# The expert output product as a sixth chunk of the last part's Strassen step

## The chip, the cores and the metric

The kernel runs on one core of a Trainium2 chip. The core has five engines with instruction streams of their own: TensorE (matmuls, PE in the profile; PEld is its weight load), VectorE (DVE), ScalarE (ACT), GpSimd (POOL) and SyncE (SP), which here only issues DMAs. The metric is the device time of one execution in microseconds. Before the change three runs took 771.34, 771.65 and 771.67 us; their median is 771.65.

## What is computed

For 2048 tokens x (width 640) the output is `g * a + (1 - g) * b`, with one gate `g` per token. Part `a` is the real part of a two-dimensional Fourier transform, written as matrix products; part `b` is a layer of 256 experts, of which every token picks two in each of 32 heads by two key scores:

```python
g = _sigmoid((x * gate_w).sum(-1, keepdims=True))
y = jnp.einsum("ts,bse->bte", dft_seq_re, a) - jnp.einsum("ts,bse->bte", dft_seq_im, b)
act = _gelu(jnp.einsum("nd,nhkd->nhk", xf, ue))
out = jnp.einsum("nhk,nhk,nhkd->nd", g, act, ve)
```

Written densely, the expert part is a matrix z (2048 tokens x 256 experts: activation times summed gate weights times 1 - g) times v (256 x 640). That last product, z times v, is what the change is about.

## The kernel before, in words

All matmuls are single-precision values split in two (`split`, lines 120 to 124): a high part made by ACT's copy and a low part made by a subtraction on POOL or VectorE. `mm3` (lines 126 to 130) then issues three 128x512 matmuls for one product, so all of them show as lines 128, 129 and 130.

The work is staged by hand in one program order. First come 128 pieces (`NPC`) of the transform along the sequence: for each of two matrices and four column chunks of 512 tokens, 16 pieces of 15 matmuls (`seq_piece`). When the 16 pieces of a chunk are done, its five banks are copied out by ACT (line 222), multiplied by the gate on VectorE (`gate_piece`, line 193) and stored to DRAM as `pd` (`store_piece`, line 203). The last of these, piece group 7, is gated in slot NPC and its five stores are issued in slot NPC+1 on SP; those of the other groups are issued on ACT. Between the pieces run the score matmuls, the picks, and `experts`, which builds the summed gate weights per expert with short TensorE products (line 653, out of tiles called hot), masked copies on ACT (line 612) and reductions on VectorE (line 618). `Pump` feeds this background work by credits, and all of it is issued before the last part begins.

What else is to be done at a certain place is registered with `at(n, f, ...)` and runs, in the order of registration, when slot n of the program has been issued (`follow`). Slots below NPC are pieces, slots from NPC on are the steps of the last part.

The last part multiplies the stored, gated partial results (4 chunks of 512 tokens, real and imaginary, 5 chunks of 128 columns as the contraction) by the transform of the width. It works in two halves b = 0, 1. In a half the left side is a 2x2 arrangement (two token chunks by real and imaginary), the right side D a 2x2 arrangement (real and imaginary by two column groups of 256), and a Strassen step with seven products forms four output quarters out of seven units instead of eight:

```python
UNITS = ("a11", "a12", "s1", "s2", "s4", "s3", "a22")
```

The last 128 columns (bank W) are left over and go along as a third product in the units a11, a12, s1 and a22. The sums on the left (s1 to s4) are made of stored sums (`pqs`) in half 0 and on VectorE (`add_a`, line 801) in half 1; the sums on the right, P, are made once by `make_sums` and `split_sums` in VectorE and POOL, for each of the 5 chunks, in the slots NPC-14 to NPC-5. `NSTEP` is the number of steps of a half, 7 units times 5 chunks; a step has 9 matmuls (with W) or 6 (s2, s4, s3). The step's operands lie in a ring of six slots and are split five steps ahead (`AHEAD`, `split_step`): by ACT and POOL, and by ACT and VectorE for s2 and s3. The first five are split in the slots NPC-4 to NPC-1 (`prep_split`).

The raw operands come by `load_a` on SP's queue into tiles that `take` hands out in a fixed order and `give` returns: 5 of the tag wf (the buffers of the pieces before), 12 of X10 to X15 (which the pieces free one by one) and 2 of xf, 19 in all; after that, returned ones.

The expert product is made beside this, without Strassen. `load_v` (NPC-3) loads v, `split_v` (NPC) splits it on ACT and VectorE and makes a negated copy of the last columns on ACT (line 765). For each of the four chunks of 512 tokens `load_z` issues eleven DMAs on SP (the gate row, line 861; the activations, line 864; the summed weights in four pieces, line 867, each for two expert halves), `split_z` multiplies them on VectorE (one operation at line 877, two each at lines 880 and 881) and splits them into `zop` by ACT and POOL. In a half, chunk 0 is loaded in slot M-1 and split at M+3 (M is the half's first slot), chunk 1 at M+21 and M+25. `z_group` issues the matmuls in four places: 18 at the end of unit a12, 12 at the end of s4, 12 after s3 (`quarter`, with its own subtraction in `post`, "q"), and 18 ahead of a22. `store_gates(1)`, which writes the second group's summed weights to DRAM, is registered at NPC+28.

The queues matter: every engine and SP's DMA queue work strictly in the order in which the program issued. A DMA whose tile is not yet free, or whose source is not yet computed, holds up all DMAs behind it on SP.

## Time and profile before

| | |
|---|---|
| median of three runs | 771.65 us |
| profiled execution | 771.14 us, its span 769.4 us |
| PE busy | 764.3 us (99%), 4125 matmuls |
| DVE, ACT, POOL busy | 544.8 us (71%), 314.0 us (41%), 333.1 us (43%) |
| granted TensorE clock | 1.000 |
| last part | from 614.94 us to 765.4 us |

The span goes from the first to the last instruction; the profiled execution's time has 1.74 us more around it. A line of a timeline has the start, the duration, the engine, the kernel's line, the operation and its operands; what stands in brackets is the idle time before it and what ended it. `x5` means that five like instructions in a row are shown as one, with the time from the first's start to the last's end. SPq is SP's DMA queue: the time of such a line is that of issuing, not of the transfer. In a table by stages each engine has its busy time and, in brackets, its instructions. A busy PE is not a PE at its peak: a matmul shows as 0.39 us and the next begins 0.23 us after it.

### The profile page before, as it was taken

How to read it: one execution, taken by the hardware profiler on the slowest of the kernel's cores; microseconds unless marked ns; L12 is line 12 of the kernel's file. 1: busy time of each engine (PE TensorE's matmuls, PEld its weight loads, DVE VectorE, ACT ScalarE, POOL GpSimd, SP SyncE). 2: the span in 40 equal slices, each digit the busy share in tenths (PEclk: the TensorE clock that was granted, in tenths of full speed). 3: DMA queues.
4: the chain of work that ended last, by engine and by line, in shares of the span. 5: the costliest groups of instructions: out<-in, count | busy, mean ns of one | idle time of the engine just before them, and what ended most of it. 6: DMA issues, size and time to landing. Idle time of an engine off the chain costs nothing.

```text
span 769.4 us, 11163 instructions
## 1 busy us (share of the span) xinstructions
PE 764.3 (99%) x4125; PEld 625.1 (81%) x4125; DVE 544.8 (71%) x628; ACT 314.0 (41%) x572; POOL 333.1 (43%) x232
## 2 busy tenths in 40 slices
PE   9999999999999999999999999999999999999997
PEld 7777777888888888888888888888888878888886
DVE  7751032289899799999899969869889862427551
ACT  5334223321223532533523675543345663424350
POOL 5423225232422323324156656334357574549270
PEclk9999999999999999999999999999999999999999
DMA  9977995403212332221353442558864677766321
GB/s 344 347 294 187 357 345 203 150 27 97 77 40 73 115 116 59 65 96 47 100 170 125 153 148 83 167 191 287 276 222 166 221 266 250 243 195 199 124 83 68
DMA packets 75654, 130.33 MB, mean 169 GB/s; under 512 B 17104, under 2 KB 24400, under 8 KB 75344
## 3 DMA queue, kind: packets, MB, share of 16 engines
q1 hardware_dynamic: 63424, 113.23, 44.5%
q10 hardware_dynamic: 12176, 16.40, 6.0%
q8 instruction: 32, 0.52, 0.3%
q14 instruction: 22, 0.18, 0.1%
HBM read 102.84 MB, written 25.17 MB: 166 GB/s over the span
## 4 chain that ended last, share of the span: by engine, by line
PE 97%; POOL 1%; DMA 1%; issue 0%; SPq 0%; DVE 0%; DVEq 0%; POOLq 0%
PE b L128 31%; PE b L130 30%; PE b L129 30%; PE b L333 2%; PE b L215 2%; PE b L653 1%; DMA ra<-pqs 1%; POOL WS L124 1%; PE b L344 1%; PE b L283 0%; POOL WP L124 0%; SPq L798 0%; DVE ST L1002 0%; DVEq L1108 0%; POOLq L124 0%
## 5 line engine op out<-in xcount | busy, mean ns | idle before, releaser
L124 POOL TENSOR_TENSOR WS<-wf,WS 128x512 fp32r<-128x512 f32 x127 | 194.0, 1531 | 258.6 <-ACT WS L123 246.5
L128 PE MATMUL b<-WS,X 128*128 128x512 f32 x620 | 244.2, 394 | 0.0
L130 PE MATMUL b<-WS,X 128*128 128x512 f32 x620 | 241.5, 389 | 0.0
L129 PE MATMUL b<-WS,X 128*128 128x512 f32 x620 | 241.4, 389 | 0.0
L128 PEld LDWEIGHTS b<-WS,X 128*128 128x128 f32 x620 | 116.3, 188 | 28.5 <-issue 4.1
L130 PEld LDWEIGHTS b<-WS,X 128*128 128x128 f32 x620 | 116.4, 188 | 24.6
L129 PEld LDWEIGHTS b<-WS,X 128*128 128x128 f32 x620 | 116.4, 188 | 23.4
L123 ACT ACTIVATE WS<-wf 128x512 fp32r<-128x512 f32 x127 | 80.2, 632 | 95.6 <-PE b L130 52.8
L642 DVE TENSOR_TENSOR hot<-rows,wtab 128x1024 f16<-128x1024 f16 x64 | 63.2, 1014 | 10.2 <-PE b L653 10.2
L438 ACT ACTIVATE sc<-b 128x512 f32<-128x512 f32 x32 | 19.8, 618 | 107.6 <-PE b L130 107.6
L128 PE MATMUL b<-WU,xh 128*128 128x512 f32 x160 | 62.3, 390 | 0.0
L129 PE MATMUL b<-WU,xh 128*128 128x512 f32 x160 | 62.3, 390 | 0.0
L130 PE MATMUL b<-WU,xl 128*128 128x512 f32 x160 | 62.2, 389 | 0.0
L124 POOL TENSOR_TENSOR xl<-xf,xh 128x640 fp32r<-128x640 f32 x16 | 25.8, 1615 | 82.8 <-ACT xh L123 78.5
L452 DVE TENSOR_REDUCE mm<-sc 128x64 f32<-128x1024 f32 x32 | 38.9, 1217 | 25.7 <-ACT sc L438 25.1
L124 POOL TENSOR_TENSOR WS<-ra,WS 128x512 fp32r<-128x512 f32 x32 | 44.6, 1410 | 25.5 <-ACT WS L123 25.3
L454 DVE TENSOR_TENSOR eq<-sc,mm 128x1024 f16<-128x1024 f32 x32 | 51.5, 1608 | 1.1
L612 ACT ACTIVATE b<-b,mask 128x128 f32<-128x128 f32 x128 | 42.6, 340 | 16.0 <-PE b L653 12.9
L347 DVE TENSOR_TENSOR WU<-b,WU 128x512 fp32r<-128x512 f32 (+1 forms) x16 | 7.9, 491 | 57.5 <-ACT WU L346 57.5
L124 POOL TENSOR_TENSOR WP<-ra,WP 128x512 fp32r<-128x512 f32 x18 | 27.6, 1543 | 34.1 <-ACT WP L123 27.8
L458 DVE TENSOR_REDUCE rr<-eq 128x64 f16<-128x1024 f16 x32 | 39.0, 1219 | 1.0
L123 ACT ACTIVATE WS<-ra 128x512 fp32r<-128x512 f32 x46 | 28.3, 631 | 25.9 <-PE b L130 13.3
(157 smaller groups left out, 1245.0 us busy)
## 6 DMA issues: line engine op xcount, KB each, us to landing
wq<-in_wq SPq DMA_DIRECT2D x32, 640.0 KB, 7.2
wf<-in_wsim SPq DMA_DIRECT2D x64, 256.0 KB, 3.5
wf<-in_wsre SPq DMA_DIRECT2D x63, 256.0 KB, 4.8
ra<-pd SPq DMA_DIRECT2D x50, 256.0 KB, 3.8
pd<-ST ACTq DMA_DIRECT2D x35, 256.0 KB, 3.1
xf<-in_xT SPq DMA_DIRECT2D x16, 320.0 KB, 3.3
ra<-pqs SPq DMA_DIRECT2D x20, 256.0 KB, 4.8
xr<-in_xn SPq DMA_DIRECT2D x15, 320.0 KB, 7.1
```

Source lines behind the costliest of these rows:

```text
L123: nc.scalar.activation(h, f, AF.Copy)
L124: eng.tensor_sub(l, f, h.bitcast(F32))
L128: nc.tensor.matmul(o, wh, ah, start=first, stop=False, skip_group_check=more)
L129: nc.tensor.matmul(o, wh, al, start=False, stop=False, skip_group_check=more)
L130: nc.tensor.matmul(o, wl, ah, start=False, stop=last, skip_group_check=more)
L215: nc.tensor.matmul(banks[d], X[s][:, x, d * P:(d + 1) * P], c, start=n + a == 0, stop=False)
L438: nc.scalar.activation(scs[i].rearrange("p h e -> p (h e)")[:, c], ps, AF.Copy)
L452: nc.vector.tensor_reduce(m, sc, op=OP.max, axis=AX.X)
L454: nc.vector.tensor_tensor(eq, sc, m[:, :, None].to_broadcast([P, HH, E]), op=OP.is_equal)
L458: nc.vector.tensor_reduce(r, eq, op=OP.max, axis=AX.X)
L612: nc.scalar.activation(f[:, :, n], f[:, :, n], AF.Copy, scale=mask4[:, n:n + 1])
L642: nc.vector.tensor_tensor(o, a, b, op=op)
```

## The change

The product of z and v becomes a sixth chunk (number KD = 5) of each of the seven units. v's two expert halves take the place of D's real and imaginary rows, and z's two expert halves that of the left side's; the sums of v take a place beside P (`make_sums(KD)`, `split_sums(KD)`, in tiles X8 and X9), and the sums of z are made by `sum_z` and `add_a` on VectorE. `z_group`, `quarter`, `zop`, the negated columns and the post step "q" go. A unit has six steps, a half 42, and the operands of chunk 5 go through the ring of six slots like the others: they are split by ACT and POOL, or VectorE for s2 and s3.

Much of the order moves with it. v is loaded at NPC-5 (from NPC-3), split at NPC-3 (from NPC) and summed at NPC-1 and NPC. z's chunk 0 is loaded at NPC-5 for half 0 (from NPC-1) and made by `make_z` at NPC-1; chunk 1 is loaded at NPC+1 (from NPC+21) and made at NPC+6. In slot NPC-5, `load_v` and `load_z` are registered ahead of `load_a` of a11's chunk 1. `store_gates(1)` moves to NPC+2. The loads of s1 begin at NPC+2 (from NPC), where they stand behind the five stores of the last gated group, behind `load_z(0, 1)` and behind `store_gates(1)`; the other loads move by the added steps. The raw tiles get four more, out of hot0, ahead of the two of xf.

```diff
-NSTEP = 7 * KD
+KZ = KD + 1
+NSTEP = 7 * KZ
...
-        return DD[:, 0, a, k, 2 * P:4 * P] if n == 3 else TS[k][:, PAIR + a * P:][:, :P]
+        return right(0, a, k)[:, 2 * P:4 * P] if n == 3 else TS[m][:, PAIR + a * P:][:, :P]
+
+    def right(w, a, k):
+        return T[("xh", "xl")[a]][:, w] if k == KD else DD[:, w, a, k]
...
-            T["t"] = big.tile([P, 9 * P], F32, name="tf", tag="xl")
+        if k in (0, KD):
+            T["t"] = big.tile([P, 9 * P], F32, name="tf", tag="X9" if k else "xl")
...
     def load_v():
-        T["f"] = big.tile([P, 2, D], F32, name="dt", tag="xf")
-        nc.sync.dma_start(T["f"], vv.rearrange("k p d -> p k d"))
+        T[KD] = big.tile([P, 2, D], F32, name="dt", tag="xf")
+        nc.sync.dma_start(T[KD], vv.rearrange("k p d -> p k d"))
 
     def split_v():
 
         for t in ("xh", "xl"):
             T[t] = big.tile([P, 2, D], F32R, name="v" + t, tag=t)
-        split(T["f"], T["xh"], T["xl"], nc.vector)
-        for a, t in enumerate(("xh", "xl")):
-            nc.scalar.activation(v_neg(a), T[t][:, :, 4 * P:], AF.Copy, scale=-1.0)
-
-    def v_neg(a):
-        return TS[5 + a][:, PAIR:].rearrange("p (k d) -> p k d", k=2)
+        for w in range(2):
+            split(T[KD][:, w], T["xh"][:, w], T["xl"][:, w], nc.vector)
 
     for k in range(KD):
         at(NPC - 17 + 2 * k, load_dt, k)
         at(NPC - 14 + 2 * k, make_sums, k)
         at(NPC - 13 + 2 * k, split_sums, k)
-    at(NPC - 3, load_v)
-    at(NPC, split_v)
-    at(NPC + 28, store_gates, 1)
-
-
-    fresh, raw_free, raw_tags = deque(), deque(), [("wf", 1)] * 5 + [(f"X{s}", 2) for s in range(10, 16)] + [("xf", 2)]
+    at(NPC - 5, load_v)
+    at(NPC - 3, split_v)
+    at(NPC - 1, make_sums, KD)
+    at(NPC, split_sums, KD)
+    at(NPC + 2, store_gates, 1)
...
+    fresh, raw_free, raw_tags = deque(), deque(), [("wf", 1)] * 5 + [(f"X{s}", 2) for s in range(10, 16)] + [("hot0", 4), ("xf", 2)]
...
-            key = (b, "s" if b and what in ("s1", "s2", "s4") else what, k)
+            key = (b, "s" if (b or k == KD) and what in ("s1", "s2", "s4") else what, k)
...
-            if b == 0 or what in ("a11", "a12", "a22", "s3", "s4"):
+            if what in ("a22", "s3", "s4") or k < KD and (b == 0 or what in ("a11", "a12")):
...
-            a, f = take((b, "za", k)), take((b, "zf", k))
+            a, f = take((b, f"a{n + 1}{k + 1}", KD)), take((b, "zf", k))
             nc.sync.dma_start(a, actd[k][:, c * TC:(c + 1) * TC])
...
-    def split_z(b, n):
-
-        if not zop:
-            for k in range(2):
-                zop[k] = big.tile([P, 2, TC], F32R, name="zo", tag=f"X{8 + k}")
+    def make_z(b, n):
+
         g = raw[b, "g", n]
-        s = -1.0 if n == 0 else 1.0
-        nc.vector.tensor_scalar(g, g, s, -s, op0=OP.mult, op1=OP.add)
+        nc.vector.tensor_scalar(g, g, -1.0, 1.0, op0=OP.mult, op1=OP.add)
         for k in range(2):
-            a, f = raw[b, "za", k], raw[b, "zf", k]
+            a, f = raw[b, f"a{n + 1}{k + 1}", KD], raw[b, "zf", k]
             nc.vector.tensor_tensor(a, a, f, op=OP.mult)
             nc.vector.tensor_tensor(a, a, g, op=OP.mult)
-            split(a, zop[k][:, 0], zop[k][:, 1], nc.gpsimd)
-            give((b, "za", k))
             give((b, "zf", k))
         give((b, "g", n))
-        bg.credit -= 3.5
+        bg.credit -= 3.0
+
+    def sum_z(b):
+        s, a21 = take((b, "s", KD)), raw.pop((b, "a21", KD))
+        nc.vector.tensor_add(s, a21, raw[b, "a22", KD])
+        nc.vector.tensor_add(a21, a21, raw[b, "a11", KD])
+        raw[b, "s3", KD] = a21
+        bg.credit -= 1.5
...
-        elif what == "q":
-            add("c22", "Y", OP.subtract)
             put(b, 1, 2, res["c22"])
...
-    def z_group(o, c0, w, first=False, last=False, more=False):
-
-        for k in range(2):
-            h, l = zop[k][:, 0], zop[k][:, 1]
-            for d in range(2):
-                c = slice((c0 + d) * P, (c0 + d + 1) * P)
-                mm3(roles[o][d], T["xh"][:, k, c], T["xl"][:, k, c], h, l, first and k == 0, last and k == 1, more)
-                run_bg(0.68)
-            if w:
-                mm3(roles["W"], w(0)[:, k], w(1)[:, k], h, l, False, last and k == 1)
-                run_bg(0.68)
...
-            if what == "a22":
-                z_group("Z", 0, v_neg, first=True)
...
-            "a11": ("X", lambda a: DD[:, 0, a, k, 0:2 * P], lambda a: DD[:, 0, a, k, 4 * P:]),
-            "a12": ("Z", lambda a: DD[:, 1, a, k, 0:2 * P], lambda a: DD[:, 1, a, k, 4 * P:]),
-            "s1": ("Y", lambda a: t_sum(k, 0, a), lambda a: DD[:, 0, a, k, 4 * P:]),
+            "a11": ("X", lambda a: right(0, a, k)[:, 0:2 * P], lambda a: right(0, a, k)[:, 4 * P:]),
+            "a12": ("Z", lambda a: right(1, a, k)[:, 0:2 * P], lambda a: right(1, a, k)[:, 4 * P:]),
+            "s1": ("Y", lambda a: t_sum(k, 0, a), lambda a: right(0, a, k)[:, 4 * P:]),
...
-            "s4": ("Y", lambda a: DD[:, 1, a, k, 2 * P:4 * P], None),
+            "s4": ("Y", lambda a: right(1, a, k)[:, 2 * P:4 * P], None),
...
-        end = k == KD - 1
+        end = k == KD
...
-            mm3(roles[o][d], w(0)[:, c], w(1)[:, c], h, l, k == 0 and what in ("a11", "a12", "s1"),
-                end and what not in ("a12", "s4"), more)
+            mm3(roles[o][d], w(0)[:, c], w(1)[:, c], h, l, k == 0 and what in ("a11", "a12", "s1", "a22"), end, more)
...
-        if what == "a12":
-            z_group("Z", 0, lambda a: T[("xh", "xl")[a]][:, :, 4 * P:], last=True)
-        if what == "s4":
-            z_group("Y", 2, None, last=True, more=True)
...
-            at(NPC + m, quarter, b)
...
                     for n, x in enumerate(held):
-                        mm3(roles["Z"][1], *x, False, n == KD - 1)
+                        mm3(roles["Z"][1], *x, n == 0, n == KD)
...
-    def quarter(b):
-        roles["Y"] = [bank(3), bank(4)]
-        z_group("Y", 2, None, first=True, last=True)
-        at(NPC + b * NSTEP + 6 * KD, post, b, "q")
-
     M = NPC
+    at(M - 5, load_z, 0, 0)
     for k in range(KD):
         at(M - 6 + k, load_a, 0, "a11", k, 1, 1)
         at(M - 4 + min(k, 3), load_a, 0, "a12", k, 1, 2)
-        at(M + k // 2, load_a, 0, "s1", k, 0, 0)
-        at(M + 2 + k, load_a, 0, "s2", k, 0, 0)
-        at(M + 7 + k, load_a, 0, "s4", k, 0, 0)
-        at(M + 12 + k, load_a, 0, "s3", k, 0, 0)
-        at(M + 18 + k, load_a, 0, "a22", k, 2, 2)
+        at(M + 2 + k // 2, load_a, 0, "s1", k, 0, 0)
+        at(M + 5 + k, load_a, 0, "s2", k, 0, 0)
+        at(M + 11 + k, load_a, 0, "s4", k, 0, 0)
+        at(M + 17 + k, load_a, 0, "s3", k, 0, 0)
+        at(M + 24 + k, load_a, 0, "a22", k, 2, 2)
     M = NPC + NSTEP
+    at(M - 6, load_z, 1, 0)
     for k in range(KD):
         at(M - 8 + k, load_a, 1, "a11", k, 1, 1)
         at(M - 4 + k, load_a, 1, "a12", k, 1, 2)
-        at(M + k, load_a, 1, "s", k, 2, 2)
...
-        at(M + 5 + k, load_a, 1, "a11", k, 1, 1)
...
-        at(M + 21 + k, load_a, 1, "a22", k, 2, 2)
...
+        at(M + 1 + k, load_a, 1, "s", k, 2, 2)
...
+        at(M + 6 + k, add_a, 1, "s", "s3", k, False)
...
+        at(M + 17 + k, add_a, 1, "s", "a12", k, True)
+        at(M + 27 + k, load_a, 1, "a22", k, 2, 2)
     for b in range(2):
         M = NPC + b * NSTEP
-        for n, i in ((0, -1), (1, 21)):
-            at(M + i, load_z, b, n)
-            at(M + i + 4, split_z, b, n)
+        at(M + 1, load_z, b, 1)
+        for n, i in ((0, -1), (1, 6)):
+            at(M + i, make_z, b, n)
+        at(M + 9, sum_z, b)
+        at(M + 15, add_a, b, "s", "a11", KD, True)
+        at(M + 21, add_a, b, "s", "a12", KD, True)
```

More of the change, by code (lines that the diff above doesn't have):

```diff
@@ L746, in split_sums @@
     def split_sums(k):
-        for n in [k] + ([5 + k // 2] if k % 2 == 0 else []):
-            TS[n] = big.tile([P, 2 * D], F32R, name="ts", tag=f"X{(1, 3, 4, 5, 6, 0, 2, 7)[n]}")
+        for n in [8] if k == KD else [k] + ([5 + k // 2] if k % 2 == 0 else []):
+            TS[n] = big.tile([P, 2 * D], F32R, name="ts", tag=f"X{(1, 3, 4, 5, 6, 0, 2, 7, 8)[n]}")
         t = T["t"]
@@ L787, in take @@
             else:
-                r = big.tile([P, 2, TC], F32, name="ra", tag=t)
-                fresh.extend(r[:, a] for a in range(2))
+                r = (p3 if t == "hot0" else big).tile([P, n, TC], F32, name="ra", tag=t)
+                fresh.extend(r[:, a] for a in range(n))
         raw[key] = f = (fresh or raw_free).popleft()
@@ L927, in post @@
             put(b, 1, 0, res["c"])
[L929 to L939 removed]
     held = []
     def step(m):
[L944 removed]
+        b, (u, k) = m // NSTEP, divmod(m % NSTEP, KZ)
         what = UNITS[u]
@@ L977, in step @@
         if w5:
-            mm3(roles["W"], w5(0), w5(1), h, l, k == 0 and what in ("a11", "s1"), end and what == "a22")
+            mm3(roles["W"], w5(0), w5(1), h, l, k == 0 and what in ("a11", "s1"),
+                end and what in ("a12", "a22"))
             run_bg(0.68)
@@ L1023, in gated_mix_kernel @@
         at(M - 4 + k, load_a, 1, "a12", k, 1, 2)
[L1024 to L1032 removed]
+        at(M + 1 + k, load_a, 1, "s", k, 2, 2)
+        at(M + 1 + k, load_a, 1, "s3", k, 2, 1)
+        at(M + 6 + k, add_a, 1, "s", "s3", k, False)
+        at(M + 7 + k, load_a, 1, "a11", k, 1, 1)
+        at(M + 11 + k, add_a, 1, "s", "a11", k, False)
+        at(M + 11 + k, add_a, 1, "s3", "a11", k, True)
+        at(M + 11 + k, load_a, 1, "a12", k, 1, 2)
+        at(M + 17 + k, add_a, 1, "s", "a12", k, True)
+        at(M + 27 + k, load_a, 1, "a22", k, 2, 2)
     for b in range(2):
         M = NPC + b * NSTEP
[L1035 to L1037 removed]
+        at(M + 1, load_z, b, 1)
[4 more added lines that the diff above has]
+        at(M + 21, add_a, b, "s", "a12", KD, True)
     prep_split = {NPC - 4: (0,), NPC - 3: (1,), NPC - 2: (2,), NPC - 1: (3, 4)}
```

14 lines of the change are left out of this document (3 added, 11 removed).

## The prediction

> **What bounds the kernel now.** I read the page first, for the span and the chain that ended last; then the table by stages for the two halves of the last part; then each engine's timeline from 600 to 640 us, the only place in the last part where TensorE waits.
>
> ```profile
> span 769.4 us, 11163 instructions
> PE 97%; POOL 1%; DMA 1%; issue 0%; SPq 0%; DVE 0%; DVEq 0%; POOLq 0%
> ra<-pqs SPq DMA_DIRECT2D x20, 256.0 KB, 4.8
> ```
>
> The chain is TensorE for 97% of the span, so a matmul that goes is worth its pitch, and a late operand is paid in full.
>
> ```profile
> 614.94:689.90 74.96, 74.61 (x329) 61.47 (x328) 29.65 (x36) 32.64 (x58) 41.63 (x31) 1.00 0.75 242
> 689.90:765.40 75.50, 75.47 (x333) 62.14 (x332) 42.44 (x51) 26.46 (x45) 37.63 (x25) 1.00 0.38 122
> ...
> 614.94 0.39 PE L128 MATMUL b<-WP,DD 128*128 128x512 f32 x1
> 615.62 0.39 PE L128 MATMUL b<-WP,DD 128*128 128x512 f32 x1
> 633.30 0.39 PE L128 MATMUL b<-WS,DD 128*128 128x512 f32 x1
> 634.04 0.50 PE L129 MATMUL b<-WS,DD 128*128 128x512 f32 x1 [0.35 <-POOL WS L124]
> 634.37 0.40 PE L130 MATMUL b<-WS,DD 128*128 128x512 f32 x1
> ```
>
> The two halves of the last part run with TensorE never idle but for 0.35 us (columns after the length: busy PE, PEld, DVE, ACT, POOL; then the granted clock, 1.00). The pitch is (615.62 - 614.94)/3 = 0.227 us. At 634 us one operand is late: 633.30 to 634.37 is 1.07 us for two pitches, so this wait costs 0.62. VectorE is busy 30 and 42 of 75 us, POOL 42 and 38: both halves have room on average. What decides is the hand-over into the last part:
>
> ```profile
> 601.90 0.40 SPq L757 DMA_DIRECT2D dt<-in_vv  x1
> 608.67 0.43 SPq L861 DMA_DIRECT2D ra<-gdr  x1
> 612.46 2.56 SPq L867 DMA_DIRECT2D ra<-gd  x4
> 615.13 0.84 SPq L798 DMA_DIRECT2D ra<-pqs  x2
> 616.93 4.93 SPq L203 DMA_DIRECT2D pd<-ST  x5
> ...
> 615.61 0.69 DVE L618 TENSOR_REDUCE cd<-b 128x128 f32<-128x512 f32 x1 [0.69 <-ACT b L612]
> 616.22 5.29 DVE L193 SCALAR_TENSOR_TENSOR ST<-ST,grow 128x512 f32<-128x512 f32 x5
> ```
>
> SP issues its DMAs in program order. Two loads of s1 go out at 615.13, ahead of the five stores of the last gated piece, which follow VectorE's gating (616.22 to 621.51) one by one; the other s1 loads follow them. So today the operands of the third unit, s1, are on chip long before they are wanted.
>
> **The change part by part.**
>
> *Matmuls.* A half has 5 chunks x (4 units x 9 + 3 units x 6) = 270 matmuls, and 60 for z:
>
> ```profile
> L128 PE MATMUL b<-zo,vxh 128*128 128x512 f32 x36 | 14.0, 389 | 0.0
> L128 PE MATMUL b<-zo,ts 128*128 128x512 f32 x4 | 1.6, 389 | 0.0
> ...
> L124 POOL TENSOR_TENSOR WS<-ra,WS 128x512 fp32r<-128x512 f32 x32 | 44.6, 1410 | 25.5 <-ACT WS L123 25.3
> ```
>
> The z rows make 3 x (36 + 4) = 120 matmuls in both halves (L129 and L130 have as many as L128). A sixth chunk costs 54 for a half, so 12 matmuls go: 12 x 0.227 = 2.72 us, all on the path.
>
> *z operands.* The eight POOL splits into zo and their ACT copies go; 14 splits of chunk 5 come, 10 on POOL and 4 on VectorE, so POOL has two more 1.41 us splits over 150 us. VectorE gains make_sums (5 operations) and three split parts once, and for each half sum_z (2 additions) and two more additions, and loses the two of the separate quarter (line 925). ACT loses the two negations (line 765). I cost these at nothing after the first 27 us: the ring of operands is split five steps ahead, at least 5 x 6 x 0.227 = 6.8 us, against some 2.1 us for one ACT copy and POOL split. If that cover went, a late split would stop TensorE for its lateness: six POOL splits of s4 in a row, 1.41 each against a step of 6 x 0.227 = 1.36, lose 0.3 us of the 6.8, and would have to be 1.1 us slower each to use it up. The z groups that gave the engines 2.7 to 4 us of rest after a12, s4 and s3 are gone, but the same five steps cover that.
>
> *v earlier.* load_v moves from NPC-3 to NPC-5 in SP's order and still waits for the tile xf, which the last make_sums frees: at 601.90, as now. What is new is what queues behind it: the eleven DMAs of load_z(0,0), and only then the loads of a11 chunks 1 to 4 and all a12.
>
> ```profile
> 649.88 1.74 SPq L867 DMA_DIRECT2D ra<-gd  x4
> ...
> DMA to landing us min/median/max: 2.1/4.3/6.7
> ...
> 611.57 1.28 ACT L222 ACTIVATE ST<-b 128x512 f32<-128x512 f32 x2 [3.13 <-PE b L130]
> 612.74 2.84 ACT L612 ACTIVATE b<-b,mask 128x128 f32<-128x128 f32 x8
> ```
>
> Bounds for eleven DMAs: 612.46 + 2.56 - 608.67 = 6.35 us above, 11 x 0.435 = 4.8 below (1.74 for four). I take 5.2. So a11 chunk 2 goes out near 607.9 and lands near 611.9 (4.0, a little under that row's median for all raw loads, as SP has just been idle). ACT, in order, copies it (0.62), then the two L222 (1.17 to the next start) and then the masks, at 613.7 in place of 612.74: **+1.0 us** on the masks and on VectorE's last reduction. Bounds 0 and 3.7 (landing 2.1 and 6.7).
>
> *The order on VectorE.* Behind that reduction (ends 616.30) stands the gating now. After the change make_sums of v and make_z(0,0), both in NPC-1, stand before it (NPC).
>
> ```profile
> L739 DVE TENSOR_TENSOR tf<-dt x5: 685/1180/1778, 567.1 to 597.6; 128x512 f32<-128x512 f32 x5
> L740 DVE SCALAR_TENSOR_TENSOR tf<-tf,dt x5: 424/426/1404, 568.9 to 599.5; 128x256 f32<-128x256 f32 x5
> L742 DVE TENSOR_TENSOR tf<-dt x5: 419/964/967, 571.1 to 600.2; 128x256 f32<-128x256 f32 x5
> L743 DVE TENSOR_TENSOR tf<-dt x5: 276/823/1382, 572.0 to 601.1; 128x128 f32<-128x128 f32 x5
> ...
> 597.62 1.77 DVE L739 TENSOR_TENSOR tf<-dt 128x512 f32<-128x512 f32 x1
> ...
> 623.94 0.41 DVE L877 TENSOR_SCALAR ra<-ra 128x512 f32<-128x512 f32 x1
> 627.41 1.67 DVE L881 TENSOR_TENSOR ra<-ra 128x512 f32<-128x512 f32 x1
> 664.05 0.42 DVE L877 TENSOR_SCALAR ra<-ra 128x512 f32<-128x512 f32 x1
> 667.40 0.69 DVE L881 TENSOR_TENSOR ra<-ra 128x512 f32<-128x512 f32 x1
> ...
> L193 DVE SCALAR_TENSOR_TENSOR ST<-ST,grow x5: 682/684/1789, 616.2 to 619.7; 128x512 f32<-128x512 f32 x5
> ```
>
> make_sums: 2.2 us from the minima (L741 as L740), 4.3 from the last one before (from 597.62 to load_v at 601.90, which waits for its end). I take 2.6, near the low end: POOL's next splits wait then for ACT, which is still at masks and L222, so nothing disturbs VectorE. make_z: 5.14 (623.94 to 629.08) and 4.04 (664.05 to 668.09); below, 0.41 + 4 x 0.68 = 3.1. I take 4.0. The gating: 5.3 as now, beside POOL's splits; 3.4 if none disturbs it (5 x 0.684, its median).
>
> *The order on SP.* The five stores wait for the gating; behind them the change puts load_z(0,1) (eleven DMAs, NPC+1) and store_gates(1) (NPC+2), and only then s1. The two s1 loads that went out before the stores lose that place.
>
> ```profile
> 654.44 1.18 SPq L593 DMA_DIRECT2D gd<-cd  x2
> ```
>
> Sum: 616.3 + 1.0 + 2.6 + 4.0 + 5.3 = 629.2; last store + 0.4; load_z 5.2; store_gates 1.2 (0.84 below, two loads at 615.13); s1 chunk 0 lands 4.0 later (4.8 above, the page's median for pqs); ACT 0.62, POOL 1.41 and hand-overs 0.1: **ready at 642.1**. TensorE wants it at its thirteenth step, 614.94 + 12 x 2.04 = 639.4. So it waits about **2.7 us**. With the low ends of all it is ready at 635.3, four us early; with all high ends at 653.7, which needs every term to go wrong together. Earlier, chunk 5 of a11 and the split of v's sums stand before a12 on ACT and POOL and may cost 0 to 1.4 us there; that wait lies inside the 2.7, since the chain of s1 doesn't depend on TensorE. ACT's copy of W (line 988) is queued behind its copy of s1 chunk 4, which lands 4 x 0.435 = 1.7 us after chunk 0, at 641.6: W is free at 641.6 + 2 x 0.62 = 642.9, and step 12 comes to it at 642.1 + 1.36 = 643.5, so this adds nothing. Tiles for the loads are not short: hot0 adds four.
>
> Sum: -2.72 for matmuls, -0.62 for the wait at 634, which the longer stretch replaces, +2.7 = **-0.6 us**. The profiled execution took 771.14 (1.74 around its span), so 770.5; the median of the runs, 771.65, stands 0.51 above it, and I carry the difference over: **771.0 us**.
>
> **The rivals.**
>
> *Covered.* s1 arrives in time or less than 1.8 us late: load_z at its fast pace (4.8), a landing of 3 us, VectorE undisturbed (make_z 3.1, gating 3.4). Four such things take 0.4 + 1 + 0.9 + 1.9 = 4.2 us away, more than the 2.7. For it: SP and the DMA engines have little else to do once the gating runs. Against: POOL's splits, which run through this stretch now as well:
>
> ```profile
> 617.67 5.00 POOL L124 TENSOR_TENSOR WS<-ra,WS 128x512 fp32r<-128x512 f32 x3 [6.68 <-ACT WS L123]
> ```
>
> Time 768.3 (all covered) to 770.1, say 769.0.
>
> *Slower: VectorE beside POOL.* If the blocks before the stores all run at their disturbed pace (make_sums 4.3, make_z 5.14, and the gating with two more of its five operations at its maximum of 1.79), they add 1.7 + 1.1 + 2.2 = 5.0 us, s1 is ready at 647.1, the wait is 7.7 and the time 776.0. It decides from 2.2 of these 5.0 us on: the wait is then 4.9, and 4.9 - 2.72 - 0.62 = 1.56 us slower. The rows speak for it, as every block here has been seen at both paces.
> [...]
>
> *v's split in the way of the last experts.* split_v, now at NPC-3, puts two 128x640 subtractions before the last products of the experts on VectorE.
>
> ```profile
> L642 DVE TENSOR_TENSOR hot<-rows,wtab 128x1024 f16<-128x1024 f16 x64 | 63.2, 1014 | 10.2 <-PE b L653 10.2
> 609.76 1.78 DVE L642 TENSOR_TENSOR hot<-hot,rows 128x1024 f16<-128x1024 f16 x1
> 612.14 0.69 PE L653 MATMUL b<-hot 128*64 128x64 f16 x32
> 621.44 2.57 DVE L124 TENSOR_TENSOR vxl<-dt,vxh 128x1280 fp32r<-128x1280 f32 x1
> ```
>
> The last product ends at 611.54, TensorE uses it at 612.14: 0.6 us of slack against up to 2.57. The wait would be 2.0 us, and moves all behind it: 773.0. Against it: POOL's splits of a11 chunks 1 and 2 move out of this stretch (their loads come later), so the last product, 1.78 us now, may take the 1.01 us that is the mean of the 64, or less, and the two subtractions less than 2.57.
>
> **How the numbers follow.** Within 0.2% (1.54 us) is about what a measurement of this kernel can't tell from no change. Forecast (wait 1.8 to 4.9 us): 0.45, its own range 770.1 to 773.2. Covered: 0.30. VectorE beside POOL: 0.18. v's split: 0.07, half of it within the bound. So faster 0.30, same 0.48, slower 0.22. The range 768.5 to 774.0 takes in nearly all of the covered case, the forecast and the third rival, and leaves out the far half of the second.
>
> **What would show it.** Right: 648 matmuls in the last part at a pitch of 0.227; the pd stores on SP ending near 629 to 630 in place of 621.9, the first pqs load at 635 to 636 in place of 615.13; a TensorE wait of 2 to 3 us at the start of s1, near 640, released by POOL's split of a raw tile; no wait of note from 660 on. Covered: no wait there. Wrong: a wait before the experts' last matmuls at 612; waits in the second half (the ring too short without the z groups); a granted clock under 1.

## The result: 1.5% slower, and the profile after

The changed kernel took 783.09 us (median of four runs, 782.22 to 783.71) against 771.5 us for the kernel before (four runs, 771.34 to 771.67). The ratio is 1.015, with an interval of 1.0135 to 1.0165. The prediction was 771.0 us with a range up to 774.0, so the forecast, its range and its likeliest sign were all wrong. The profiled execution of the changed kernel took 782.22 us with a span of 780.2.

Lines in the changed kernel stand one higher than before: the split is at L124 and L125, the three matmuls are L129 to L131, the masked copies L613, the gating L194, the stores of pd L204.

The page of the changed kernel: span, TensorE's work, the granted clock in 40 slices, and the chain by engine.

```profile
span 780.2 us, 11187 instructions
PE 766.6 (98%) x4113; PEld 624.6 (80%) x4113; DVE 558.3 (72%) x645; ACT 320.1 (41%) x582; POOL 337.2 (43%) x236
...
PEclk9999999999999999999999999999999997999999
...
PE 95%; DMA 2%; SPq 1%; DVE 1%; issue 1%; POOL 0%; ACT 0%; DVEq 0%; ACTq 0%; POOLq 0%
```

The matmuls fell from 4125 to 4113, as the change says. Yet TensorE's busy time rose by 2.3 us and one slice has a lower clock. The chain that ended last now has DMA, SP's queue and VectorE in it for 2%, 1% and 1% of the span. The table by stages of the changed kernel (length; busy PE, PEld, DVE, ACT, POOL with their instructions; granted clock, DMA share, GB/s) says where:

```profile
614.82:643.00 28.18, 25.16 (x107) 19.48 (x106) 22.15 (x24) 12.46 (x29) 17.27 (x12) 1.00 0.46 150
643.00:648.30 5.30, 0.76 (x4) 0.30 (x2) 3.51 (x6) 0.63 (x1) 0.00 (x0) 0.86 0.94 277
648.30:657.20 8.90, 7.66 (x17) 5.23 (x18) 1.20 (x1) 4.27 (x7) 7.50 (x6) 0.51 1.00 347
657.20:690.00 32.80, 32.80 (x146) 27.15 (x145) 10.10 (x15) 15.54 (x27) 11.53 (x10) 1.00 0.81 269
```

The last part starts at 614.82, against 614.94 before. From 657 us on TensorE is never idle. All that was lost was lost in between, in three forms: short waits up to 643, a long wait from 643, and some ten microseconds at half the clock. TensorE's waits from 600 us on in the changed kernel (total, times, longest), and then its timeline at the places that count:

```profile
PE b L129 <- ACT WP L124: 4.6, 1, 4.6
PE b L130 <- POOL WP L125: 2.2, 2, 1.6
PE b L130 <- POOL WS L125: 1.3, 2, 1.0
PE b L129 <- ACT ST L970: 0.7, 1, 0.7
```
```profile
627.48 0.50 PE L130 MATMUL b<-WS,vxh 128*128 128x512 f32 x1 [0.95 <-POOL WS L125]
631.45 0.50 PE L130 MATMUL b<-WP,DD 128*128 128x512 f32 x1 [1.60 <-POOL WP L125]
643.37 0.39 PE L131 MATMUL b<-WS,vxl 128*128 128x512 f32 x1
648.32 0.79 PE L129 MATMUL b<-WP,ts 128*128 128x512 f32 x1 [4.56 <-ACT WP L124]
649.67 0.80 PE L130 MATMUL b<-WP,ts 128*128 128x512 f32 x1 [0.56 <-POOL WP L125]
650.69 0.63 PE L129 MATMUL b<-WP,ts 128*128 128x512 f32 x1
651.12 0.63 PE L130 MATMUL b<-WP,ts 128*128 128x512 f32 x1
652.84 0.80 PE L129 MATMUL b<-WP,DD 128*128 128x512 f32 x1 [0.67 <-ACT ST L970]
```

At 648.32 unit s1 begins; a little further on two matmuls in a row start 651.12 - 650.69 = 0.43 us apart in place of 0.227. I count a loss as the time from one matmul's start to the next over 0.227. Added up over the last part this gives 14.0 us: 4.1 before s1 (0.39 at 615, 0.62 at 622, 1.23 at 627, 1.87 at 631) and 9.9 from 643.4 to 657.2. Against this stand the 2.72 us of the matmuls that went and the 0.62 of the wait that the kernel before had at 634. 14.0 - 2.72 - 0.62 = 10.7, and the spans differ by 780.2 - 769.4 = 10.8. So the account closes, and the question is only why s1's operands came at 648 to 650 in place of the 642.1 that was forecast, and what the 4.1 us and the half clock are.

SP's queue in the changed kernel, which answers to the five lines of it shown of before (time of issuing, not of transfer):

```profile
602.27 0.42 SPq L862 DMA_DIRECT2D ra<-gdr  x1
...
606.20 2.63 SPq L868 DMA_DIRECT2D ra<-gd  x4
...
628.00 5.98 SPq L204 DMA_DIRECT2D pd<-ST  x5
634.08 1.55 SPq L862 DMA_DIRECT2D ra<-gdr  x1
...
638.52 2.06 SPq L868 DMA_DIRECT2D ra<-gd  x4
640.62 1.18 SPq L594 DMA_DIRECT2D gd<-cd  x2
641.84 1.87 SPq L801 DMA_DIRECT2D ra<-pqs  x1
```

The order is the one that the prediction gives: stores, load_z(0,1), store_gates, and only then s1. But the first s1 load goes out at 641.84, when it had been expected at 635 to 636, and it takes 1.87 us to issue, the second 1.78 and the next three 0.49, 0.38 and 0.38, so that the fifth is issued at 646.69. VectorE, ACT and POOL in the changed kernel, for the steps up to the stores:

```profile
618.50 0.69 DVE L619 TENSOR_REDUCE cd<-b 128x128 f32<-128x512 f32 x1 [0.69 <-ACT b L613]
619.11 0.68 DVE L744 TENSOR_TENSOR tf<-dt 128x512 f32<-128x512 f32 x1
622.13 1.51 DVE L874 TENSOR_SCALAR ra<-ra 128x512 f32<-128x512 f32 x1
626.21 7.43 DVE L194 SCALAR_TENSOR_TENSOR ST<-ST,grow 128x512 f32<-128x512 f32 x5
```
```profile
611.89 0.63 ACT L124 ACTIVATE WP<-ra 128x512 fp32r<-128x512 f32 x1 [3.35 <-DMA ra<-pd]
614.13 0.63 ACT L124 ACTIVATE WS<-ra 128x512 fp32r<-128x512 f32 x1 [1.61 <-DMA ra<-pd]
615.62 2.85 ACT L613 ACTIVATE b<-b,mask 128x128 f32<-128x128 f32 x8
...
625.06 0.63 ACT L124 ACTIVATE WS<-ra 128x512 fp32r<-128x512 f32 x1 [4.06 <-DVE ra L878]
...
647.64 0.63 ACT L124 ACTIVATE WP<-ra 128x512 fp32r<-128x512 f32 x1 [13.00 <-DMA ra<-pqs]
```
```profile
625.77 1.66 POOL L125 TENSOR_TENSOR WS<-ra,WS 128x512 fp32r<-128x512 f32 x1 [2.42 <-ACT WS L124]
```

ACT works in order, and at 625.06 it has stood 4.06 us for the last operation of make_z, whose result is chunk 5 of a11. POOL stood behind it, and from 625.77 to 638.96 splits without a pause, over the whole of the gating.

### The profile page after: what moved, and what is told of

The parts are those of the page before. It is cut to its first block, busy times and chain, and to the rows that moved or that the text cites. A ratio compares the mean times of both kernels' runs of the same rounds, so it can differ in the third digit from the quotient of the medians.

```text
span 780.2 us, 11187 instructions
## 1 busy us (share of the span) xinstructions
PE 766.6 (98%) x4113; PEld 624.6 (80%) x4113; DVE 558.3 (72%) x645; ACT 320.1 (41%) x582; POOL 337.2 (43%) x236
## 4 chain that ended last, share of the span: by engine, by line
PE 95%; DMA 2%; SPq 1%; DVE 1%; issue 1%; POOL 0%; ACT 0%; DVEq 0%; ACTq 0%; POOLq 0%
PE b L129 30%; PE b L130 29%; PE b L131 29%; PE b L334 2%; PE b L216 2%; PE b L654 1%; DMA ra<-pd 1%; SPq L801 1%; DMA ra<-pqs 1%; PE b L345 1%; DMA ra<-actd 1%; PE b L284 0%; POOL WP L125 0%; DVE ra L874 0%; DVE tf L748 0%
## 5 line engine op out<-in xcount | busy, mean ns | idle before, releaser
L125 POOL TENSOR_TENSOR WS<-wf,WS 128x512 fp32r<-128x512 f32 x127 | 193.5, 1527 | 260.8 <-ACT WS L124 251.6
L129 PE MATMUL b<-WS,X 128*128 128x512 f32 x620 | 244.2, 394 | 0.0
L131 PE MATMUL b<-WS,X 128*128 128x512 f32 x620 | 241.5, 390 | 0.0
L129 PEld LDWEIGHTS b<-WS,X 128*128 128x128 f32 x620 | 116.3, 188 | 28.6 <-issue 4.1
L131 PEld LDWEIGHTS b<-WS,X 128*128 128x128 f32 x620 | 116.4, 188 | 24.5
L124 ACT ACTIVATE WS<-wf 128x512 fp32r<-128x512 f32 x127 | 80.2, 631 | 95.2 <-PE b L131 49.9
L125 POOL TENSOR_TENSOR WS<-ra,WS 128x512 fp32r<-128x512 f32 x40 | 55.8, 1412 | 16.4 <-ACT WS L124 16.1
L129 PE MATMUL b<-WU,xh 128*128 128x512 f32 x160 | 62.3, 390 | 0.0
L131 PE MATMUL b<-WU,xl 128*128 128x512 f32 x160 | 62.2, 389 | 0.0
L125 POOL TENSOR_TENSOR xl<-xf,xh 128x640 fp32r<-128x640 f32 x16 | 25.7, 1609 | 80.9 <-ACT xh L124 76.7
L124 ACT ACTIVATE WS<-ra 128x512 fp32r<-128x512 f32 x56 | 35.0, 631 | 50.5 <-PE b L131 32.1
L125 POOL TENSOR_TENSOR WP<-ra,WP 128x512 fp32r<-128x512 f32 x20 | 29.3, 1480 | 59.8 <-ACT WP L124 59.8
L613 ACT ACTIVATE b<-b,mask 128x128 f32<-128x128 f32 x128 | 42.7, 340 | 16.3 <-PE b L654 13.2
```

The source lines that it names most:

```text
L124: nc.scalar.activation(h, f, AF.Copy)
L125: eng.tensor_sub(l, f, h.bitcast(F32))
L129: nc.tensor.matmul(o, wh, ah, start=first, stop=False, skip_group_check=more)
L131: nc.tensor.matmul(o, wl, ah, start=False, stop=last, skip_group_check=more)
L613: nc.scalar.activation(f[:, :, n], f[:, :, n], AF.Copy, scale=mask4[:, n:n + 1])
```

## The experiments

Two theories stood at the start. A: s1's loads are late because of the order on SP, and this makes the long wait and what follows from it. B: the loads are late whatever their place, since the DMA engines are full in this stretch (share 0.94 to 1.00). Beside them stood three smaller questions: what the clock costs, where the early 4.1 us come from, and whether the 12 matmuls are worth what was computed.

**s1's loads back in their old slots.** The first two loads of s1 go ahead of the five stores again, the other three behind the stores but ahead of load_z(0,1) and store_gates(1).

```diff
-        at(M + 2 + k // 2, load_a, 0, "s1", k, 0, 0)
+        at(M + (k > 1), load_a, 0, "s1", k, 0, 0)
```

> The changed kernel with one thing moved: the five loads of s1 go out on SP ahead of load_z(0,1) and store_gates(1), two of them ahead of the five stores (slots NPC and NPC+1 in place of NPC+2 to NPC+4). Theory A, SP's order: s1's loads are late only because they queue behind the stores, load_z and store_gates; the 4.7 us of idle TensorE at the start of s1 and the half clock after it go together, 9.9 us by the sum of the matmul gaps, and what is left are the 4.1 us of waits before s1: 773.2 (772.5 to 775). Rival B, the transfers themselves: at 640 to 657 us the DMA engines are 0.92 to 1.00 busy, so s1, s2 and z are late together whatever their order: a wait of 3 us or more stays in s1 or s2, 777 or more.

It took 773.38 us against 770.85, a ratio of 1.0032 (1.0018 to 1.0046). SP's queue in this kernel:

```profile
615.66 0.96 SPq L801 DMA_DIRECT2D ra<-pqs  x2
628.84 5.99 SPq L204 DMA_DIRECT2D pd<-ST  x5
634.88 2.63 SPq L801 DMA_DIRECT2D ra<-pqs  x3
```

The stores are as late as in the changed kernel (628.84), load_z(0,1) now stands behind s1, and TensorE doesn't wait at s1 at all. Its waits are the early ones alone, and the granted clock of the run is 1.00:

```profile
PE b L130 <- POOL WP L125: 1.6, 1, 1.6
PE b L130 <- POOL WS L125: 1.3, 2, 1.0
PE b L129 <- ACT ST L223: 1.1, 1, 1.1
```

One line of order holds some 9 of the 11.6 us. Theory A holds and B falls as the cause: the same bytes, ordered otherwise, stop nobody.

**Only the fifth load late.** As above, but chunk 4 of s1 stays behind load_z(0,1) and store_gates(1). The prediction said that the copy of W, queued on ACT behind that chunk's copy, "adds nothing".

```diff
-        at(M + 2 + k // 2, load_a, 0, "s1", k, 0, 0)
+        at(M + (k > 1) + (k > 3), load_a, 0, "s1", k, 0, 0)
```

> e1_s1_first, but with the fifth load of s1 (chunk 4) left behind load_z(0,1) and store_gates(1). ACT copies in order: chunk 4 of s1 stands ahead of the copy of bank W, which the first step of s1 needs. Theory A': the W product of s1's first step waits until chunk 4 has landed (issued near 645, landed near 649.5, W copied near 651) in place of 645: a wait of 4 us or more there, with the clock falling, 777 to 781. Rival (the prediction's sum, by which W adds nothing): chunk 4 is wanted only at the seventeenth step, near 653: the time of e1_s1_first, 772.5 to 774.

781.18 us, a ratio of 1.0129 (1.0111 to 1.0148). 7.4 of the 9 us are back, with four of the five loads early. ACT and TensorE in this kernel:

```profile
650.34 0.63 ACT L124 ACTIVATE WS<-ra 128x512 fp32r<-128x512 f32 x1 [9.48 <-DMA ra<-pqs]
650.88 0.58 ACT L970 ACTIVATE ST<-b 128x512 f32<-128x512 f32 x1
```
```profile
651.51 0.80 PE L129 MATMUL b<-WP,DD 128*128 128x512 f32 x1 [5.93 <-ACT ST L970]
```

ACT stands 9.48 us before the split of chunk 4, and behind it the copy that empties bank W waits too. TensorE stops in the *first* step of s1 because of an operand of the fifth. So s1's first step needs not only the first of the five loads but, through the order on ACT, the last.

**Useless matmuls in the wait.** Into bank 7, which is free there, 20 matmuls are put ahead of s1's first product and some more ahead of its product for W; their results are used nowhere. The first of the two kernels has 13 there, the second 4.

```diff
+    def fill(n):
+        if n:
+            t = bank(7)
+            for _ in range(n):
+                nc.tensor.matmul(t, DD[:, 0, 0, 0, 0:P], DD[:, 0, 0, 0, 0:TC], start=True, stop=True)
...
     def step(m):
...
+        fill(20 if m == 12 else 0)
         for d in range(1 if very_last else 2):
...
+        fill(4 if m == 12 else 0)
         if w5:
```

> The changed kernel with 33 matmuls added that compute nothing that is used (into a bank of their own, from tiles that are there): 20 ahead of the thirteenth step, 13 ahead of that step's W product. They only fill the time in which TensorE waits. Theory A, the idle time lowers the clock: granted clock 1.00 throughout, no matmul at 0.43 us pitch; W still waits for ACT's copy at 652.8, so only the matmuls after it gain, some 10 at 0.2 us: 781.0 (780 to 782), so more matmuls and less time. Rival C, the slow matmuls from 648 to 657 are slow for their operands (late splits or loads) and not for the clock: no gain, 783 or up to 7 us more.

The first took 781.64 us against 770.85 (ratio 1.0137, 1.0122 to 1.0152). No matmul has the wide pitch any more, but the 13 ran 2.0 us beyond the moment at which W was free, so the gain and that cost can't be separated in it. Hence the second, beside the changed kernel once more on the same chip:

> e2_fill with 4 in place of 13 matmuls ahead of the W product, as 13 lasted 2.0 us beyond ACT's copy of W. Theory A (the clock): granted clock 1.00, no wait of note at W, 1.5 to 2.0 us below e2_fill against the same kernel before, and 2 to 3 us below the changed kernel. Rival C: without the long filling the pitch of 0.43 us comes back: no gain.

> The changed kernel once more, to stand beside the two others on the same chip: 783 (782 to 784), 11.6 us above the kernel before, clock 0.99.

The second took 780.2 us (ratio 1.0123, 1.0109 to 1.0136), the changed kernel 782.06 (1.0148, 1.0134 to 1.0162), both against 771.02. The same fourteen microseconds in a table by stages, first with the useless matmuls, then of the changed kernel:

```profile
643.00:657.00 14.00, 12.96 (x56) 10.03 (x55) 6.01 (x8) 5.53 (x9) 7.97 (x6) 1.00 1.00 337
```
```profile
643.00:657.00 14.00, 8.64 (x24) 5.88 (x23) 5.11 (x7) 4.89 (x8) 7.43 (x6) 0.76 0.99 324
```

With 24 more matmuls TensorE gets through 32 useful ones there in place of 24, and the kernel is 1.9 us faster. The two intervals just overlap, so this size is uncertain by about a microsecond; the traces give much the same, as from s1's second matmul to the first of its third step it is 5.38 us with the filling and 7.45 without. That is what the half clock costs here; the other 8 us of the s1 loss are the late operands themselves, the wait for W among them:

```profile
651.17 1.07 PE L935 MATMUL b<-DD 128*128 128x512 f32 x4
652.43 0.50 PE L129 MATMUL b<-WP,DD 128*128 128x512 f32 x1 [0.20 <-ACT ST L978]
```

At full clock the products ahead of W are issued by 651.17, and W is free at 652.43, 1.3 us later.

**z's first loads behind a11 and a12.** load_z(0,0) is put in slot NPC-1 again, which is behind the loads that ACT's order waits for.

```diff
-    at(M - 5, load_z, 0, 0)
+    at(M - 1, load_z, 0, 0)
```

> The changed kernel with load_z(0,0) issued in slot NPC-1, behind all loads of a11 and a12, as in the kernel before (NPC-5 in the change). Theory A: the masks return from 615.6 to 612.7, VectorE's gating, the five stores and s1's loads come 2.9 us earlier, the waits of 0.4 and 0.6 us in a11 go, those at chunk 5 (1.2 and 1.9) shrink; since s1's wait ends 2.9 us earlier, 780.2 (779 to 781). Rival: the early waits only hand their time on to s1's wait and the stores don't move, as z now lands later and make_z waits for it: 782 to 784.

778.41 us, a ratio of 1.0097 (1.0082 to 1.0112), 1.8 us under the time that was expected. VectorE in this kernel:

```profile
623.27 7.47 DVE L194 SCALAR_TENSOR_TENSOR ST<-ST,grow 128x512 f32<-128x512 f32 x5
```

The masks are back where they were before the change (612.67, and 612.74 then). The early losses shrink from 4.1 us to 0.2, since a11's and a12's operands are split in time, and the whole chain to the s1 loads moves up by 2.9 us (gating at 623.27 against 626.21, s1 loads from 638.91). The long wait at s1 stays (5.0 us, and 9.2 in all with the half clock). The other terms of that chain stay as well, though a11 and a12 are in time here: the gating takes 7.47 us against 7.43, load_z(0,1) 6.5 us as before, and from the first s1 load to its copy on ACT it is 6.2 us against 5.8. A new wait appears: the experts' last matmuls are split in two, and the last part begins at 615.98. This is the prediction's third rival, and I come back to it.

**v's sums later.** make_sums and split_sums of v go behind the gating.

```diff
-    at(NPC - 1, make_sums, KD)
-    at(NPC, split_sums, KD)
+    at(NPC + 6, make_sums, KD)
+    at(NPC + 7, split_sums, KD)
```

> The changed kernel with make_sums and split_sums of v seven slots later (NPC+6 and NPC+7 in place of NPC-1 and NPC), behind the gating on VectorE and behind chunk 5 and a12's first splits on ACT and POOL. Theory A: make_z and the gating start 3.1 us earlier, the stores and s1's loads too, and the split of a12's first chunk no longer waits for POOL's two sums (1.9 us wait): 780.0 (778.5 to 781). Rival: VectorE's order doesn't matter, because SP is bound by its own DMAs: 782.5 or more.

780.2 us, a ratio of 1.0121 (1.0106 to 1.0136). The time is the expected one, but not by the way that was expected. The gating starts at 624.89, 1.3 us earlier and not 3.1, for make_z takes 5.1 us here in place of 4.1 and the reduction ahead of it ends 0.7 later; the gating itself takes 8.57 us in place of 7.43, and the last store is issued only 0.2 us earlier. What did come is that 1.6 us are lost before s1 in place of 4.1, as fewer copies and splits stand ahead of a12. In the profiled run, the slowest of the four with 781.55, most of this only makes TensorE wait longer at s1, 6.2 us in place of 4.6.

**Both orders, and all three.** The first two edits on s1 and z together, and then with v's sums later as well:

> The changed kernel with both loads put back in order: s1's five ahead of load_z(0,1) (as in e1_s1_first) and load_z(0,0) behind those of a11 and a12 (as in e3_z_after_a). Theory A: the two removed every wait of the last part's start between them (9.9 us by the one, 3.9 by the other), so what is left is the change's own saving: 770.85 - 2.7 for 12 matmuls - 0.6 for the old wait = 767.5 (767 to 768.5), faster than the kernel before. Rival D, the room is gone: with the z groups away the ring runs dry in s1 to a22 or in the second half, and some wait of 1 us or more stays: 769 to 772.

> e5_s1_and_z with v's sums seven slots later too (as in e4_sums_late). Theory A: once s1's loads no longer queue behind VectorE's gating, VectorE's order is off the path: the time of e5_s1_and_z within 0.5 us, though the sums alone gave some 3 us in e4_sums_late. Rival: VectorE's order is worth time by itself: 1 us or more below e5_s1_and_z; or, as the second z now waits for a tile that the sums hold, 1 us or more above.

With two edits 769.44 us against 771.27 (ratio 0.9977, 0.9968 to 0.9986); with three 769.15 (0.9974, 0.9964 to 0.9983). Both beat the kernel before, and with s1's loads early the order on VectorE is worth 0.3 us, less than the runs can tell. But 767.5 had been expected of the two, and 1.9 us were missing, 0.4 of them because the kernel before was that much slower beside these runs. The rest is not the shortage of the ring that the rival supposed, for in the last part TensorE loses only 0.1 us over its pitch. It lies ahead of the last part. VectorE and TensorE in the kernel with three edits:

```profile
608.88 1.54 DVE L125 TENSOR_TENSOR vxl<-dt,vxh 128x640 fp32r<-128x640 f32 x2
610.35 1.78 DVE L643 TENSOR_TENSOR hot<-rows,wtab 128x1024 f16<-128x1024 f16 x1
612.05 1.76 DVE L643 TENSOR_TENSOR hot<-hot,rows 128x1024 f16<-128x1024 f16 x1
```
```profile
612.55 0.44 PE L654 MATMUL b<-hot 128*64 128x64 f16 x16
613.87 0.32 PE L654 MATMUL b<-hot 128*64 128x64 f16 x8 [0.88 <-ACT b L613]
```

The two subtractions for v stand ahead of the experts' last two products, and these take 1.78 and 1.76 us, beside POOL, which splits a11's chunks from 609.65 to 613.27. The product is late, the short matmuls come in pieces, and the last part begins at 616.41. In the changed kernel itself a11's loads were so late that POOL was idle there, from 607.29 to 612.60; the same two products took 0.68 each, and nothing was to be seen.

**v's split elsewhere.** Two ways to take it out of the products' way: two slots later, or on POOL in place of VectorE, both with the three edits.

```diff
-    at(NPC - 3, split_v)
+    at(NPC - 1, split_v)
```

> e6_s1_z_sums with split_v in slot NPC-1 in place of NPC-3, behind the experts' last products on VectorE. In e6_s1_z_sums the last part began at 616.4 in place of 614.9, after a wait of 1.0 us of the experts' last matmuls for their operands and 0.3 around it. Theory A (the third rival of the prediction): v's split, 1.54 us on VectorE, stands ahead of those products, and shows once POOL's splits run beside them; with it behind them the last part begins near 615.0 and the time falls by 1.3 us below e6_s1_z_sums: near 767.9, 3.3 us below the kernel before. Rival: it only moves the 1.54 us to chunk 5 of a11, which needs v and z: within 0.4 us of e6_s1_z_sums.

771.41 us, a ratio of 1.0003 (0.9994 to 1.0012): a miss by 3.5. The last part begins 0.8 us earlier, but the subtractions for v now stand on VectorE ahead of make_z and the gating, which starts at 625.15 in place of 621.71, and TensorE has waits at 626 (0.48), 642 (1.01), 652 (0.70) and 680 (1.39). The one at 642 is for W again: ACT stands there for v's sums, which VectorE makes behind the gating, and copies W only at 642.27. The work was moved onto the next thing that is waited for.

```diff
-            split(T[KD][:, w], T["xh"][:, w], T["xl"][:, w], nc.vector)
+            split(T[KD][:, w], T["xh"][:, w], T["xl"][:, w], nc.gpsimd)
```

> e6_s1_z_sums with v's split on POOL in place of VectorE (two 128x640 subtractions, some 1.6 us each by POOL's other ones), so that VectorE has only the experts' last products there. Theory A: the experts' matmuls no longer wait 1.0 us, the last part begins 1.2 us earlier and nothing else moves, as POOL has 5 us free before its third split of a11: 768.0, some 3 us below the kernel before. Rival: POOL's splits beside the products slow these as much as the split of v did (1.78 in place of 0.68 us each): the wait stays and the time is that of e6_s1_z_sums, 2 us below the kernel before.

768.0 us (767.9 to 768.73, five runs) against 771.04, a ratio of **0.9965** (0.9951 to 0.9978). POOL, and TensorE's waits over the whole span in this kernel:

```profile
608.00 3.54 POOL L125 TENSOR_TENSOR vxl<-dt,vxh 128x640 fp32r<-128x640 f32 x2 [0.75 <-ACT vxh L124]
```
```profile
PE b L284 <- PEq L1085: 0.8, 1, 0.8
```

POOL is slower at it (3.54 us against 1.54), and no one waits for it there. The experts' last two products are still slow beside POOL (1.79 and 2.05 us), as the rival had it, but they start 2.0 us earlier than in the kernel with three edits, and that is enough. The experts' matmuls run in one piece at 611.99, the last part begins at 614.79, and in it TensorE loses nothing over its pitch; the one wait left in the whole kernel is that ahead of its first matmul. The gain is 3.04 us; the prediction's two savings make 2.72 + 0.62 = 3.34.

## Why the prediction was wrong, step by step

**The matmuls: right.** 12 fewer are in the page, and the last kernel shows that they and the old wait at 634 are worth what was computed, within 0.3 us.

**The mechanism of the loss: right in kind and place, far off in size.** "The order on SP" is the failed step: it gave "ready at 642.1" and a wait of "about 2.7 us". TensorE's first matmul that needs both parts of s1's chunk 0 began at 649.67, 7.6 us later. The terms of its sum against the trace:

| term | predicted | measured | from |
|---|---|---|---|
| VectorE's last reduction ends | 617.3 | 619.19 | 618.50 + 0.69 |
| make_sums of v | 2.6 | 3.1 | 619.11 to 622.21 |
| make_z | 4.0 | 4.1 | 622.13 to 626.21 |
| gating and last store | 5.7 | 7.8 | 626.21 to 633.98 |
| load_z(0,1) | 5.2 | 6.5 | 634.08 to 640.58 |
| store_gates | 1.2 | 1.2 | 1.18 |
| landing | 4.0 | 5.8 | 641.84 to 647.64 |
| ACT, POOL, hand-overs | 2.1 | 2.0 | 647.64 to 649.67 |

The excess is 1.9 + 0.5 + 0.1 + 2.1 + 1.3 + 1.8, no term being shorter by more than 0.1. The rest of the miss lies behind 649.67: from there to 657.66 TensorE took 7.99 us for seventeen pitches, which are 3.86 us. These 4.1 us are the half clock and the wait for W, and the sum had put both at nothing. 7.6 + 4.1 = 11.7, and the profiled execution took 782.22 us in place of the 770.5 of the forecast.

The four large terms came out near or beyond the upper ends that the prediction had itself (3.7 for the masks, 6.35 for load_z, 4.8 for the landing, 5.3 + 2.2 for the gating). It took them from the middle or below, and held that all high ends at once "needs every term to go wrong together". The traces show something else beside each of them, and only the first was tested by a run:

- The masks came late because the first load_z, with v's load ahead of it and a11's loads behind it, took 6.6 us in place of 5.2. With load_z moved back the last reduction ends 2.9 us earlier.
- The gating ran beside POOL from its start to its end, since chunk 5 of a11, which make_z has just finished, holds up ACT and POOL until then. It isn't the lateness of a11's and a12's loads: with these in time the gating still took 7.47 us.
- load_z(0,1) and the landing hold slow issues behind stores. The first DMA of load_z took 1.55 us to issue, directly behind the five stores, and the first s1 load 1.87, directly behind store_gates. At the 0.435 of the forecast they would have been 1.1 and 1.4 us shorter. The kernel before has the same behind its store_gates, in a row next to the one from which the prediction took the 1.18: the two loads that follow took 1.73 and 2.10 us.

How the gating runs with POOL at work beside it and without, the traces show. In the kernel before, the 19 gating operations (L193) that had no POOL operation beside them took 0.68 us each (0.676 to 0.684), and the 21 that had one beside them for some or all of their time 0.68 to 2.07. In the changed kernel the five of the last group had POOL's splits beside them throughout and took 1.22 to 1.77 each, 7.43 / 5 = 1.49 from one to the next; in the kernel with three edits, where POOL has no pause either, that is 1.72 (8.58 / 5). Why an operation beside POOL takes the one pace or the other, no run shows.

**"0 to 1.4 us" for chunk 5 and v's sums: too small, but it didn't add.** 4.1 us were lost before s1, 1.2 of them at chunk 5 and 1.9 at a12's first chunk; the other 1.0 earlier in a11. As the prediction says, this lies inside the lateness of s1, whose chain doesn't depend on TensorE. In the kernel with s1's loads first nothing hides it: there TensorE loses 5.2 us over its pitch in the last part, all of it before s1, and is 0.3% slower than before in spite of the 12 matmuls.

**"VectorE gains ... I cost these at nothing after the first 27 us": right.** There is no wait from 660 us on, and the ring's five steps cover the added work in both halves.

**W "adds nothing": wrong.** The step put the landing of chunk 4 1.7 us behind that of chunk 0, at the quiet issue time. With the two slow issues ahead of it chunk 4 went out 4.85 us behind chunk 0, and ACT's copies of the two start 4.03 us apart (647.64 and 651.67). TensorE idled 0.67 us for it in the changed kernel; at full clock, as in the kernel with the short filling, it is 1.3. The kernel with only the fifth load late shows that the dependence alone can bring back most of the loss.

**The rivals.** "VectorE beside POOL" (0.18) came nearest: its place and its sign were right, and its 776.0 too low. But of the three blocks that it raised only the gating ran at the disturbed pace; make_sums and make_z stayed near the forecast's 2.6 and 4.0. So 2.7 us of the 7.6 are VectorE's, and 5.0 are the masks, load_z(0,1) and the landing, which this rival left at their middles. That the sign came out as it says is in part luck. The range left out its far half, and that is where the time fell. The half clock, for which its sum has no term, came with the wait of 4.56 us. "v's split in the way of the last experts" (0.07) did not show in the changed kernel, and cost about 1.5 us as soon as the orders were mended. "Covered" (0.30) rested on four terms at their fast pace; none of the four was.

## What to carry to other kernels

When a block of DMAs is moved on an in-order queue, find every load that falls behind it, and what stands in order behind each of these loads on the engine that uses it. Here one line that put five loads back ahead of the block was worth 9 us, and the last of the five alone 7.4. Take the price of an issue from a row that has the same neighbours: 0.4 us from a quiet stretch was 1.9 behind a block of stores. Where an operation has been seen at two paces, ask what will run beside it in the new order, before taking a value in between. And when an order is mended, look for the next engine with work ahead of something waited for: 3 us of saved matmuls came out only when the last such place, a split on VectorE, had gone to an engine with room.

## What the runs showed of the hardware

The granted TensorE clock fell to half after one long wait in the middle of a kernel that was busy for 640 us before: 0.51 over 648.3 to 657.2, a pitch of 0.43 us in place of 0.227, after 4.56 us idle. Five traces here have an idle stretch of 4 us or more (4.10, 4.56, 4.97, 5.93 and 6.22 us), and all five show it; in the others the longest was 1.64 us, and none does. What an idle time between 1.64 and 4.10 us does, no run shows. In the changed kernel, read in slices of 1 us, the clock is 1.00 up to 646, 0.92 in the next slice and 0.50 from 647: it fell 3.1 us after the idle time began, and stayed at half for 10.2 us. After the waits of 4.10 and 4.97 TensorE was already at work again when it fell: the first matmul took 0.49 and 0.51 us, the second 0.80 in both. There the half clock lasted some 6.7 us (a mean of 0.76 over 643 to 657, and of 0.63 over 645.8 to 655). After the wait of 5.93 the mean was 0.53 over 651.5 to 658, and after that of 6.22 the pitch stayed wide until 657.1, 9.7 us after the wait. With 24 useless matmuls in the wait the clock was 1.00 over 643 to 657.

DMA issue on SP has two paces as well. In the kernel before, this DMA follows the two of store_gates (at 654.44, shown in the prediction):

```profile
655.72 1.73 SPq L798 DMA_DIRECT2D ra<-pd  x1
```

The next one takes 2.10, and the three behind these 0.38 to 0.42. In the changed kernel the first two loads behind store_gates take 1.87 and 1.78 us and the next three 0.49, 0.38 and 0.38; with z's first loads behind a11 and a12 the first two take 3.82 together. Behind the five stores, the first DMA takes 1.55 us in the changed kernel and the second 1.76 with z's first loads moved back, but in the kernel before the first two take 0.32 and 0.42. Why, no run shows. A price per DMA taken from a quiet stretch was a lower bound here.
